# A block with Fourier mixing and a spatial gate on one core: chunks of the streamed operand made in pairs, operands moved to multiples of 512 bytes, element-wise work moved to VectorE

## The chip, the cores and the metric

One core of one Trainium2 chip runs the whole kernel. The metric is the device time of one launch in microseconds (us), median of several runs. TensorE does the matrix products, VectorE (DVE), ScalarE (ACT) and GpSimd (POOL) do element-wise work, SyncE (SP) issues most of the transfers. All data are fp32; matrix products run on fp32r operands.

## The reference

With x of 2048 x 512 (S x D), c of 512, and F/2 = 896 (FH):

```
mod = silu(c) @ w_mod, cut in six rows of 512: sa, ca, ga, sb, cb, gb
h = layernorm(x) * (1 + ca) + sa
x = x + ga * (Cr @ (h @ Hr^T) - Ci @ (h @ Hi^T))          # Cr, Ci 2048 x 2048; Hr, Hi 512 x 512
h = layernorm(x) * (1 + cb) + sb
z = gelu(h @ w_in)                                         # 2048 x 1792, halves z1, z2 of 896
g = w_sp @ layernorm(z2) + b_sp[:, None]                   # w_sp 2048 x 2048
out = x + gb * ((z1 * g) @ w_out)                          # w_out 896 x 512
```

## The kernel before

**Three matmuls for one.** Every operand is split in a high part rounded to fp32r and the rest (lo = value - high). `matmul3` (L93) issues three matmuls: high x high (L95), a second (L96) and a third (L97) with one low part each. The high part is made on ACT (L201 for the streamed operand), the low part by a DVE subtraction (L210).

**Chunks.** All streamed matrices go through one pipeline of 272 chunks of 128 x 512. A block of four chunks is loaded by SP into a `stage` tile (two buffers, L159). `prep_hi` (L184) turns one chunk with a DVE transpose in 32 x 32 squares (L173, or L193 in the z2 stage) into a tile `t` (two buffers) and has ACT copy it to `ah` (four buffers); `prep_lo` (L206) subtracts on DVE into `al` (three buffers). The loop calls `prep(n)` (L177) ahead of the matmuls of chunk n: it makes t and ah of chunk n + 3 and al of chunk n + 2. When a block's fourth chunk has been turned, its buffer is given to block b + 2.

**Stages**, in order of n, 16 to 128 chunks each:
- `mm_a` (L376), chunks 0 to 127: gp = h^T @ Cr^T (or Ci^T), 12 matmuls for one chunk; h is stationary, the chunk moves. The first four chunks (L387) run all high parts first. After each of the eight sums the result is split into `gh`, `gl` (pool `gtpool`).
- `mm_y` (L464), among them: y = g @ H, `gh` and `gl` stationary (128 columns of a 512-wide tile at a time), `hth`/`htl` moving: 384 matmuls. The rows mod 1 and 0 are folded into H through three small column tiles `col0..2` of 4 floats, which lie in pool `htpool` (L265 to L286).
- `mm_z1` (L522), 16 chunks of 21 matmuls: w_in's first half stationary.
- `mm_z2` (L538), 16 chunks of 24 matmuls of 448 columns: the chunk is stationary, w_in's second half moves, in two halves of 448 columns that lie behind one another in tiles of 896.
- `mm_w` (L618), 112 chunks: w_sp @ z2 in seven block products (Strassen's scheme), in the order 1, 6, 7, 4, 5, 3, 2, 16 chunks (eight k by two r) each. Products 1, 6, 4 and 2 take 12 matmuls for one chunk, 7, 5 and 3 take 9. They add up in PSUM banks `4 r + f`; 1, 5 and 2 start anew ("fresh"). After the last k of 1, 6, 7 and 4, `keep_w` (L633) copies banks to SBUF on ACT; after 5, 3 and 2, `add_w` (L642) adds them to such a copy on DVE. Product 4 needs `sum_t14` (L600) on DVE.
- `mm_o` (L709), the tail: 16 tiles of 21 matmuls, u = z1 * g split (L686, L692) as moving or stationary parts, then `add_o` (L704) adds x and stores.

**What sets the order.** The program is emitted by hand; each engine runs its own instructions in that order. `at(n, f, ...)` (L123) hangs a function on step n, and `run(n)` (L126) emits it behind the matmuls of that step (in the z stages ahead of them). On POOL run `add_bs` (L654, adds b_sp to g), `scale_wo` (L671, w_out times gb), a few others and the stores of intermediate results. `load_wo` (L667) has two buffers, and comes in products 3 and 2; `load_z1` (L658) brings z1 back, `make_u` (L663) multiplies on DVE.

**Where tiles lie.** Pools are stacked from both ends of SBUF. On the right come `edge` (which ends at a multiple of 512 bytes), `htpool`, `rows`, `gtpool`. A tile of 4 floats takes 32 bytes, so the three columns put 96 bytes into `htpool`: in the built program `gh0_0_0` starts at byte 142240 = 277 x 512 + 416, `ones_r` at 189344 = 369 x 512 + 416, while `hth0_1` (189952 = 371 x 512), `ah`, `hh`, `wih` and `uh` start at multiples of 512. `lines` (L72) is a tile that only takes room.

Of the kernel before, what the change touches and what calls it, by code (L numbers as in the profile page):

```python
# [13 lines left out]
P = 128  # L14
EPS = 1e-5
LINES = 160
# [3 lines left out]
def fnet_gmlp_kernel(  # L20
# [125 lines left out]
    stage, T, AH, AL = {}, {}, {}, {}  # L146
# [28 lines left out]
    prepared = set()  # L175

    def prep(n):  # L177

        if n not in prepared:
            prepared.add(n)  # L180
            prep_hi(n + 3)
            prep_lo(n + 2)

    def prep_hi(n, eng=None):  # L184
        if n >= NE:
            return
        b, k = divmod(n, 4)
        T[n] = blocks.tile([P, Q], F32, tag="t", bufs=2, name=f"t{n}")
        if n >= N4:
            squares(T[n], stage[b][:, k % 2], k // 2)  # L190
        elif N3 <= n < N4:

            nc.vector.transpose(T[n].rearrange("p (k a i) -> p a k i", k=4, i=32),  # L193
                                stage[b][:, :, 32 * k:32 * k + 32].rearrange("p (a k) i -> p a k i", k=4))
        else:
            squares(T[n], stage[b], k)
        AH[n] = blocks.tile([P, Q], F32R, tag="ah", bufs=4, name=f"ah{n}")
        if eng:
            eng.tensor_scalar(AH[n], T[n], 1.0, None, op0=ALU.mult)
        else:  # L200
            nc.scalar.activation(AH[n], T[n], AF.Copy)  # L201
        if k == 3:
            stage.pop(b)
            load(b + 2)

    def prep_lo(n):  # L206
        if n >= NE:
            return
        AL[n] = blocks.tile([P, Q], F32R, tag="al", bufs=3, name=f"al{n}")
        nc.vector.tensor_tensor(AL[n], T.pop(n), AH[n].bitcast(F32), op=ALU.subtract)  # L210
# [42 lines left out]
    WB, WT, COL = {}, {}, {}  # L253
# [11 lines left out]
    def load_columns(j):  # L265
        pl, tag = (hpre, "hraw") if j else (spool, "wb")
        WB[j] = pl.tile([P, 16, P], F32, tag=tag, bufs=1, name=f"wb{j}")
        load_block(WB[j], quad(w_mod, 0, j))
        COL[j] = htpool.tile([P, ND], F32, name=f"col{j}")

    def weigh_column(j, k):
        pl, tag = (spool, "wt") if k % 2 else (rows, "y")
        WT[j, k] = pl.tile([P, D], F32, tag=tag, bufs=1, name=f"wt{j}_{k}")
# [8 lines left out]
    def scale_columns():  # L282
        col = COL[1]
        nc.vector.tensor_scalar(col, col, 1.0, None, op0=ALU.add)
        COL[2] = htpool.tile([P, ND], F32, name="col2")
# [228 lines left out]
    def make_wi(e, k):  # L514
        wi_hi[e, k] = wpool[1 - e].tile([P, FH], F32R, name=f"wih{e}_{k}")
        wi_lo[e, k] = wpool[1 - e].tile([P, FH], F32R, name=f"wil{e}_{k}")
# [21 lines left out]
    def mm_z2(ns):  # L538
# [6 lines left out]
        for q in range(8):  # L545
            r, e = divmod(q, 2)
            ts, cols = slice(r * P, (r + 1) * P), slice(e * ZP, (e + 1) * ZP)
            for k, th, tl in a:
                matmul3(ZT[q][:, :ZP], th[:, ts], tl[:, ts], wi_hi[1, k][:, cols], wi_lo[1, k][:, cols],
# [68 lines left out]
    def mm_w(n):  # L618
# [11 lines left out]
        if k == 7:  # L630
            {1: keep_w, 6: keep_w, 7: keep_w, 4: keep_w}.get(p, add_w)(p, r)

    def keep_w(p, r):  # L633
# [5 lines left out]
        for f in range(G[p, r].shape[1]):  # L639
            nc.scalar.activation(G[p, r][:, f, :], GW[r, f], AF.Copy)  # L640

    def add_w(p, r):  # L642

        g = G[{5: 7, 3: 6, 2: 1}[p], r]
        for f in range(g.shape[1]):
# [8 lines left out]
    def add_bs(p, r, f):  # L654
        g = G[p, r][:, f, :]
        nc.gpsimd.tensor_tensor(g, g, wor["bs", r if p in (1, 6) else 2 + r], op=ALU.add)  # L656

    def load_z1(p, r):  # L658
        f0, f1 = (0, 4) if p in (1, 4) else (4, NF)
        Z1T[p, r] = gpool[0].tile([P, 4, Q], F32, tag="z1t", bufs=2, name=f"z1t{p}_{r}")[:, :f1 - f0]  # L660
# [6 lines left out]
    def load_wo(f):  # L667
        wor[f] = opool[0].tile([P, D], F32, tag="wor", bufs=2, name=f"wor{f}")
        nc.sync.dma_start(wor[f], w_out[f * P:(f + 1) * P, :])

    def scale_wo(f):  # L671
        nc.gpsimd.tensor_tensor(wor[f], wor[f], mods[5], op=ALU.mult)

    def make_wo(f):
        wo_hi[f] = opool[0].tile([P, D], F32R, name=f"woh{f}")
        wo_lo[f] = opool[0].tile([P, D], F32R, name=f"wol{f}")
# [63 lines left out]
    hi_h(0)  # L740
    prep_hi(0, nc.vector)
    prep_lo(0)
    lo_h(0)
    norm_x(1)
    hi_h(1)
    prep_hi(1)
    stats_first(2)
    prep_lo(1)
    lo_h(1)
    norm_x(2)  # L750
    prep_hi(2)
    hi_h(2)
    stats_first(3)
    norm_x(3)
    at(0, lo_h, 2)
# [59 lines left out]
    for t in range(NQ):  # L815
        n = 8 * NQ * (t + 1)
        for i in range(4):
# [37 lines left out]
    def change_s():  # L855
        p2.close()
        spre.append(ctx.enter_context(pool("spre", "right")))
        bpool.append(ctx.enter_context(pool("bpool", "right")))

# [5 lines left out]
    at(N2 + 5, change_s)  # L865
# [22 lines left out]
    zpool.append(ctx.enter_context(pool("zpool1", "right")))  # L888
# [23 lines left out]
    opool = []  # L912

    def change_g():
        wstack.close()
        gpool.append(ctx.enter_context(pool("gpool")))
        load_bs()
# [6 lines left out]
    for r in range(2):  # L924
        for f in range(4):
            at(NB[6] + 2 + 4 * r + f, add_bs, 1, r, f)
            at(NB[5] + 2 + 8 * r + 2 * f, add_bs, 4, r, f)
            if f < 3:
                at(NB[7] + 2 + 3 * r + f, add_bs, 6, r, f)
                at(NB[4] + 2 + 3 * r + f, add_bs, 7, r, f)  # L930
    at(NB[3] + 1, change_o)
    at(NB[2] - 10, load_z1, 4, 0)
    at(NB[2] - 9, load_z1, 7, 0)
    for f in range(4):
        at(NB[2] - 2 + f, make_u, 4, 0, f)
        at(NB[2] + 6 + f, make_u, 4, 1, f)
        if f < 3:
            at(NB[2] + 3 + f, make_u, 7, 0, f)
            at(NB[2] + 11 + f, make_u, 7, 1, f)
    at(NB[2] + 3, load_z1, 4, 1)  # L940
    at(NB[2] + 7, load_z1, 7, 1)
    for f in range(NF):
        n = NB[3] + 2 + 2 * f
# [72 lines left out]
```

## Time and profile before

| what | before |
|---|---|
| time, median of 3 runs | 965.48 us (965.05 to 965.58) |
| span of the profiled execution | 963.8 us |
| PE busy | 953.3 us (4196 matmuls) |
| DVE busy | 691.8 us |
| ACT busy | 369.6 us |
| POOL busy | 219.0 us |
| bytes moved | 161.27 MB |

The span runs from the first to the last instruction of one profiled execution; the page gives no other time of it. The runs' median is 1.7 us longer than this span. Matmuls are pipelined: one is listed with some 0.39 us, but the next starts sooner, so that the distance between starts ("pitch" below) is what a matmul costs. In a timeline row, the bracket at the end is the idle time before the instruction and who ended it.

### The profile page before, as it was taken

The page shows a single profiled execution, that of the slowest core. Times are in us where ns is not written, and L with a number is a line of the kernel's source. Part 1 is how long each engine was busy: PE and PEld are TensorE (multiplying, and loading weights), DVE is VectorE, ACT ScalarE, POOL GpSimd, SP SyncE. Part 2 cuts the span into 40 slices and gives each one's busy share as a digit, 9 for nine tenths or more (in the row PEclk, how much of TensorE's full clock was granted, in tenths as well). Part 3 has the DMA queues.
Part 4 walks back from the last instruction along what each step waited for, and adds up shares of the span by engine and source line. Part 5 has one row for each costly group of instructions (what it writes and reads, how often), then busy time and mean ns, then how long its engine had stood idle before and what let it go on. Part 6 is the DMA issues. An engine that isn't in the chain of part 4 may idle for free.

```text
span 963.8 us, 12355 instructions
## 1 busy us (share of the span) xinstructions
PE 953.3 (99%) x4196; PEld 788.8 (82%) x4196; DVE 691.8 (72%) x1085; ACT 369.6 (38%) x630; POOL 219.0 (23%) x363
## 2 busy tenths in 40 slices
PE   8999999999999999999999999999999999999998
PEld 5888888888888888888888999888888888778886
DVE  7789957785566767856555576888689698897642
ACT  4594424231232212322344356643444444342221
POOL 2330000111520345114323343213304230210000
PEclk9999999999999999999999999999999999999999
DMA  9996652666446787994678964545454456764441
GB/s 212 221 212 133 130 137 62 175 172 165 133 110 148 222 252 226 286 241 111 211 279 295 278 219 126 131 110 120 100 120 100 98 123 165 184 171 178 130 149 60
DMA packets 249535, 161.27 MB, mean 167 GB/s; under 512 B 130176, under 2 KB 218240, under 8 KB 249344
## 3 DMA queue, kind: packets, MB, share of 16 engines
q1 hardware_dynamic: 236800, 122.72, 53.1%
q0 software_dynamic: 11424, 37.24, 10.7%
q8 instruction: 33, 0.54, 0.2%
q10 hardware_dynamic: 1248, 0.52, 0.2%
q14 instruction: 30, 0.25, 0.1%
HBM read 123.73 MB, written 36.70 MB: 166 GB/s over the span
## 4 chain that ended last, share of the span: by engine, by line
PE 93%; DVE 3%; DMA 2%; issue 1%; SPq 1%; ACT 0%; POOL 0%; ACTq 0%; DVEq 0%
PE gp L95 12%; PE gp L96 12%; PE gp L97 12%; PE gw L97 8%; PE gw L96 8%; PE gw L95 8%; PE yp L96 3%; PE yp L95 3%; PE yp L97 3%; PE z2p L97 3%; PE z2p L96 3%; PE z2p L95 3%; PE z1p L96 3%; PE op L97 3%; PE z1p L97 3%; PE op L95 3%
## 5 line engine op out<-in xcount | busy, mean ns | idle before, releaser
L201 ACT ACTIVATE ah<-t 128x512 fp32r<-128x512 f32 x271 | 171.4, 632 | 452.9 <-DVE t L173 259.6
L210 DVE TENSOR_TENSOR al<-t,ah 128x512 fp32r<-128x512 f32 x272 | 192.9, 709 | 135.7 <-PE gp L96 50.4
L95 PE MATMUL gp<-ah,hh 128*128 128x512 f32 x496 | 193.3, 390 | 0.0
L96 PE MATMUL gp<-al,hh 128*128 128x512 f32 x496 | 193.3, 390 | 0.0
L97 PE MATMUL gp<-ah,hl 128*128 128x512 f32 x496 | 193.2, 389 | 0.0
L173 DVE STREAM_TRANSPOSE t<-stage 128x512 f32<-128x512 f32 x256 | 180.3, 704 | 11.3 <-DMA stage<-in_A_dft_seq_re_dram 5.0
L97 PE MATMUL gw<-ah,bl 128*128 128x512 f32 x400 | 156.6, 392 | 1.2 <-DVE bl L616 1.2
L95 PE MATMUL gw<-ah,bh 128*128 128x512 f32 x400 | 156.3, 391 | 1.0 <-DVE g L646 1.0
L96 PE MATMUL gw<-al,bh 128*128 128x512 f32 x400 | 156.4, 391 | 0.4 <-DVE al L210 0.4
L95 PEld LDWEIGHTS gp<-ah,hh 128*128 128x128 f32 x496 | 93.1, 188 | 19.9
L97 PEld LDWEIGHTS gp<-ah,hl 128*128 128x128 f32 x496 | 93.1, 188 | 19.7
L96 PEld LDWEIGHTS gp<-al,hh 128*128 128x128 f32 x496 | 93.1, 188 | 19.4
L97 PEld LDWEIGHTS gw<-ah,bl 128*128 128x128 f32 x400 | 75.4, 189 | 18.0 <-DVE bl L616 2.3
L95 PEld LDWEIGHTS gw<-ah,bh 128*128 128x128 f32 x400 | 75.5, 189 | 17.0 <-ACT woh L677 1.4
L96 PEld LDWEIGHTS gw<-al,bh 128*128 128x128 f32 x400 | 75.4, 189 | 16.7 <-DVE al L210 0.8
L656 POOL TENSOR_TENSOR g<-g,bs 128x512 f32<-128x512 f32 x28 | 44.4, 1619 | 118.0 <-ACT g L640 118.0
L588 POOL DMA_DIRECT2D s_d<-sj x64 | 35.3, 551 | 125.1 <-DVE sj L580 92.4
L96 PE MATMUL yp<-htl,gh 128*128 128x512 f32 x128 | 51.1, 399 | 0.0
L95 PE MATMUL yp<-hth,gh 128*128 128x512 f32 x128 | 50.4, 394 | 0.0
L97 PE MATMUL yp<-hth,gl 128*128 128x512 f32 x128 | 50.1, 392 | 0.0
L96 PE MATMUL z2p<-wil,ah 128*128 128x448 f32 x128 | 46.7, 365 | 0.0
L95 PE MATMUL z2p<-wih,ah 128*128 128x448 f32 x128 | 46.7, 365 | 0.0
(148 smaller groups left out, 1341.4 us busy)
## 6 DMA issues: line engine op xcount, KB each, us to landing
stage<-in_A_dft_seq_im_dram SPq DMA_DIRECT2D x64, 256.0 KB, 5.3
sj<-in_B_w_sp_dram SPq DMA_DIRECT2D x32, 512.0 KB, 7.5
s_d<-sj POOLq DMA_DIRECT2D x64, 256.0 KB, 3.9
stage<-s_d SPq DMA_DIRECT2D x128, 128.0 KB, 2.8
stage<-in_A_dft_seq_re_dram SPq DMA_DIRECT2D x60, 256.0 KB, 4.8
stage<-in_B_w_sp_dram SPq DMA_DIRECT2D x96, 128.0 KB, 3.3
stage<-h_d SPq DMA_DIRECT2D x32, 256.0 KB, 5.6
z_d<-z POOLq DMA_DIRECT2D x28, 256.0 KB, 8.0
```

The costliest lines, as they stand in the source:

```text
L95: nc.tensor.matmul(acc, ah, bh, start=first, stop=False, skip_group_check=go_on)
L96: nc.tensor.matmul(acc, ah, bl, start=False, stop=False, skip_group_check=go_on)
L97: nc.tensor.matmul(acc, al, bh, start=False, stop=last, skip_group_check=go_on)
L173: nc.vector.transpose(dst.rearrange("p (b i) -> p b i", i=32), block[:, :, 32 * k:32 * k + 32])
L201: nc.scalar.activation(AH[n], T[n], AF.Copy)
L210: nc.vector.tensor_tensor(AL[n], T.pop(n), AH[n].bitcast(F32), op=ALU.subtract)
L588: nc.gpsimd.dma_start(s_d[m, r, g][b * P:(b + 1) * P, :], a)
L656: nc.gpsimd.tensor_tensor(g, g, wor["bs", r if p in (1, 6) else 2 + r], op=ALU.add)
```

## The change

- **Pairs.** `t`, `ah` and `al` become three fixed tiles `ts` (2 slots), `ahs` and `als` (4 slots each). At odd n, `turn_two` turns chunks n + 3 and n + 4 with one DVE transpose (two in the z2 stage); at every n ACT makes ah of n + 3; at even n one DVE subtraction of 128 x 1024 makes al of n + 2 and n + 3. A block's buffer is handed on one step earlier. The first four chunks are turned one by one ahead of the loop, chunk 3 among them, so that the first pair's subtraction (chunks 2 and 3) is emitted at n = 0.
- **Places.** The columns move from `htpool` to `cpool`, and `lines` shrinks from 160 to 64 bytes, which keeps what follows in `cpool`'s stack at its place. w_in's second half is laid out as two halves in slots of 512 floats. `z1rows` moves to the right stack, `wt` to the ring of `rows`, `z1t` to `opool`, and w_out's tiles to a pool `wopool` of their own.
- **Engines.** b_sp: for products 7 and 4, `keep_w` becomes a DVE addition of the PSUM bank and b_sp (14 instructions) instead of an ACT copy with a POOL addition; for 1 and 6 the addition (14) runs on DVE in the tail. `scale_wo` (7) runs on DVE.
- **Times.** w_out is loaded, scaled and split during product 6. `make_u` of 4 and 7: the half r = 0 late in product 2, the half r = 1 in the first steps of the tail; the last `add_w` of product 2 also moves into the tail.
- **Banks.** Product 5 uses banks 3 r + f, product 2 uses 6, 7, 0, 1 for r = 0 and 2 to 5 for r = 1, the tail 6 and 7.

```diff
-LINES = 160
+LINES = 64
...
     def prep(n):
         if n not in prepared:
             prepared.add(n)
+            if n % 2:
+                turn_two(n + 3)
             prep_hi(n + 3)
-            prep_lo(n + 2)
+            if n % 2 == 0:
+                prep_lo(n + 2)
+
+    def slot(n, m=1):
+        return ts[:, n % 2:n % 2 + m, :]
...
+    def turn_two(n):
+        if n >= NE:
+            return
+        b, k = divmod(n, 4)
+        st = stage[b]
+        if n >= N4:
+            nc.vector.transpose(slot(n, 2).rearrange("p r (b i) -> p r b i", i=32),
+                                st[:, :, :, 16 * k:16 * k + 32])
+        elif n >= N3:
+            for m in range(k, k + 2):
+                nc.vector.transpose(slot(n + m - k)[:, 0].rearrange("p (k a i) -> p a k i", k=4, i=32),
+                                    st[:, :, 32 * m:32 * m + 32].rearrange("p (a k) i -> p a k i", k=4))
+        else:
+            nc.vector.transpose(slot(n, 2).rearrange("p k (b i) -> p k b i", i=32),
+                                st[:, :, 32 * k:32 * k + 64].rearrange("p b (k i) -> p k b i", k=2))
+        if k == 2:
+            stage.pop(b)
+            load(b + 2)
...
+        AH[n] = ahs[:, n % 4, :]
...
-    def prep_lo(n):
+    def prep_lo(n, m=2):
         if n >= NE:
             return
-        AL[n] = blocks.tile([P, Q], F32R, tag="al", bufs=3, name=f"al{n}")
-        nc.vector.tensor_tensor(AL[n], T.pop(n), AH[n].bitcast(F32), op=ALU.subtract)
+        lo = als[:, n % 4:n % 4 + m, :]
+        nc.vector.tensor_tensor(lo, slot(n, m), ahs[:, n % 4:n % 4 + m, :].bitcast(F32), op=ALU.subtract)
...
-    WB, WT, COL = {}, {}, {}
+    WB, WT = {}, {}
+    COL = {j: cpool.tile([P, ND], F32, name=f"col{j}") for j in range(3)}
...
+        if e:
+            wi_hi[e, k], wi_lo[e, k] = [wpool[0].tile([P, 2, 512], F32R, name=f"wi{m}{e}_{k}")[:, :, :ZP] for m in "hl"]
...
-                GW[r, f] = bank(4 * r + f, f"gw{p}_{r}_{f}")
+                k_ = 4 * r + f if p == 1 else 3 * r + f if p == 5 else (6, 7, 0, 1, 2, 3, 4, 5)[4 * r + f]
+                GW[r, f] = bank(k_, f"gw{p}_{r}_{f}")
...
-            nc.scalar.activation(G[p, r][:, f, :], GW[r, f], AF.Copy)
+            if p in (1, 6):
+                nc.scalar.activation(G[p, r][:, f, :], GW[r, f], AF.Copy)
+            else:
+                nc.vector.tensor_tensor(G[p, r][:, f, :], GW[r, f], wor["bs", 2 + r], op=ALU.add)
...
-        nc.gpsimd.tensor_tensor(wor[f], wor[f], mods[5], op=ALU.mult)
+        nc.vector.tensor_tensor(wor[f], wor[f], mods[5], op=ALU.mult)
...
     norm_x(3)
+    turn_one(3)
+    stage.pop(0)
+    load(2)
     at(0, lo_h, 2)
...
-    at(NB[2] - 10, load_z1, 4, 0)
-    at(NB[2] - 9, load_z1, 7, 0)
+    at(NB[3] + 3, load_z1, 4, 0)
+    at(NB[3] + 4, load_z1, 7, 0)
...
-        n = NB[3] + 2 + 2 * f
-        at(n, load_wo, f)
-        at(n + 4, scale_wo, f)
-        at(n + 6, make_wo, f)
-        at(n + 7, make_wo_lo, f)
+        n = NB[6] + 2 * f
+        at(n - 4, load_wo, f)
+        at(n + 1, scale_wo, f)
+        at(n + 1, make_wo, f)
+        at(n + 2, make_wo_lo, f)
     order = [(t, i) for t in (2, 3, 0, 1) for i in range(4)]
+    later = {0: [(make_u, 4, 1, 0), (make_u, 4, 1, 1), (add_w, 2, 0, [2])],
+             1: [(make_u, 4, 1, 2), (make_u, 4, 1, 3), (add_w, 2, 0, [3]), (load_z1, 1, 0)],
+             2: [(make_u, 7, 1, 0), (make_u, 7, 1, 1), (make_u, 7, 1, 2), (load_z1, 6, 0)],
+             3: [(add_w, 2, 1, [0, 1])], 4: [(add_w, 2, 1, [2, 3])]}
+    for n, p, r in ((3, 1, 0), (5, 6, 0), (7, 1, 1), (9, 6, 1)):
+        for f in range(4 if p == 1 else 3):
+            later.setdefault(n + f // 2, []).extend([(add_bs, p, r, f), (make_u, p, r, f)])
...
-        mm_o(*order[o], o % 2)
+        mm_o(*order[o], 6 + o % 2)
```

More of the change, by code (lines that the diff above doesn't have):

```diff
@@ L175, in fnet_gmlp_kernel @@
     prepared = set()
+    ts = blocks.tile([P, 2, Q], F32, name="ts")
+    ahs = blocks.tile([P, 4, Q], F32R, name="ahs")
+    als = blocks.tile([P, 4, Q], F32R, name="als")
     def prep(n):
@@ L514, in make_wi @@
     def make_wi(e, k):
-        wi_hi[e, k] = wpool[1 - e].tile([P, FH], F32R, name=f"wih{e}_{k}")
-        wi_lo[e, k] = wpool[1 - e].tile([P, FH], F32R, name=f"wil{e}_{k}")
+        if e:
+            wi_hi[e, k], wi_lo[e, k] = [wpool[0].tile([P, 2, 512], F32R, name=f"wi{m}{e}_{k}")[:, :, :ZP] for m in "hl"]
+            wraw[e, k] = wraw[e, k].rearrange("p (h f) -> p h f", h=2)
+        else:
+            wi_hi[e, k], wi_lo[e, k] = [wpool[1].tile([P, FH], F32R, name=f"wi{m}{e}_{k}") for m in "hl"]
         nc.scalar.activation(wi_hi[e, k], wraw[e, k], AF.Copy)
@@ L858, in change_s @@
         bpool.append(ctx.enter_context(pool("bpool", "right")))
+        zpool.append(ctx.enter_context(pool("zpool1", "right")))
+        zrow.append(w0.enter_context(pool("z1rows", "right")))
     def change_q():
```

114 lines of the change are left out of this document (44 added, 70 removed).

## The prediction

> **What bounds the kernel now.** I read the head of the page, then its chain, then TensorE's waits, then its timeline.
>
> ```profile
> span 963.8 us, 12355 instructions
> PE 953.3 (99%) x4196; PEld 788.8 (82%) x4196; DVE 691.8 (72%) x1085; ACT 369.6 (38%) x630; POOL 219.0 (23%) x363
> ```
>
> ```profile
> PE 93%; DVE 3%; DMA 2%; issue 1%; SPq 1%; ACT 0%; POOL 0%; ACTq 0%; DVEq 0%
> ```
>
> TensorE is busy 99% of the span and is 93% of the chain. So only two things shorten this kernel: a smaller distance between the starts of matmuls (the pitch), or fewer holes. DVE work that is merely saved is worth nothing unless a hole ends on it.
>
> ```profile
> PE gw L97 <- DVE bl L616: 1.2, 2, 1.0
> PE gw L95 <- DVE g L646: 1.0, 1, 1.0
> ```
>
> ```profile
> 606.17 0.39 PE L95 MATMUL gw<-ah,bh 128*128 128x512 f32 x1
> 700.09 0.39 PE L95 MATMUL gw<-ah,bh 128*128 128x512 f32 x1
> 703.49 0.39 PE L95 MATMUL gw<-ah,bh 128*128 128x512 f32 x1
> 839.53 0.63 PE L95 MATMUL gw<-ah,bh 128*128 128x512 f32 x1
> 841.66 0.63 PE L97 MATMUL gw<-ah,bl 128*128 128x512 f32 x1
> 883.75 0.39 PE L95 MATMUL op<-woh,uh 128*128 128x512 f32 x1
> ```
>
> The rows 700.09 and 703.49 are 15 matmuls apart: pitch 226.7 ns. The 1200 matmuls of the products would take 272.0 us at that pitch. They take 883.75 - 606.17 = 277.6 us, so 5.5 us are lost there. The waits give only 2.6 us of it; the rest is after-effect: behind the hole at product 2's start the pitch is 426 ns (839.53 to 841.66, five matmuls), nearly double, for about 3 us.
>
> Why is DVE late there? From the timelines of SP, DVE and POOL:
>
> ```profile
> 829.78 3.16 SPq L669 DMA_DIRECT2D wor<-in_B_w_out_dram  x2
> 832.99 4.84 SPq L157 DMA_DIRECT2D stage<-in_B_w_sp_dram  x8
> 833.50 0.71 DVE L173 STREAM_TRANSPOSE t<-stage 128x512 f32<-128x512 f32 x1 [0.94 <-DMA stage<-in_B_w_sp_dram]
> 833.87 1.30 POOL L672 TENSOR_TENSOR wor<-wor,mod 128x512 f32<-128x512 f32 x1 [6.21 <-DMA wor<-in_B_w_out_dram]
> 834.14 1.58 DVE L210 TENSOR_TENSOR al<-t,ah 128x512 fp32r<-128x512 f32 x1
> ```
>
> SP stands in front of `load_wo`, whose two buffers are still in use, and the stage loads queue behind it: a transpose waits for data. Then a subtraction runs beside POOL's `scale_wo` and takes 1.58 us. Alone it takes 0.6:
>
> ```profile
> 858.26 0.68 DVE L680 TENSOR_TENSOR wol<-wor,woh 128x512 fp32r<-128x512 f32 x1
> 858.86 0.70 DVE L173 STREAM_TRANSPOSE t<-stage 128x512 f32<-128x512 f32 x1
> 859.49 0.65 DVE L210 TENSOR_TENSOR al<-t,ah 128x512 fp32r<-128x512 f32 x1
> ```
>
> (DVE pitches 0.60 and 0.63 us.) Last, product 2 starts in the very banks that product 3's additions must first empty (the wait on L646 above).
>
> **Part 1, places of operands.** The pitch of other matmuls:
>
> ```profile
> 430.14 0.24 PE yp L96
> 432.94 0.24 PE yp L96
> ```
>
> The first two are pieces of the chain in order of time; the next two are groups of instructions:
>
> ```profile
> L95 PE MATMUL gp<-ah,hh 128*128 128x512 f32 x496 | 193.3, 390 | 0.0
> L303 PE MATMUL modp<-ws,ones_r 128*128 128x512 f32 x4 | 1.6, 394 | 0.0
> ```
>
> yp: 2.80 us for 12 matmuls, 233.3 ns, so 6.6 more than 226.7. Its moving `hth` starts at a multiple of 512 bytes; its stationary `gh` starts 416 behind one, because of the columns. modp, moving aligned and stationary `ones_r` off by 416, is long too (394 against 390). gp, gw and op, with both aligned, are not. So I blame the stationary operand's place. With the columns gone `gh` lies at a multiple of 512: 384 x 6.6 ns = **-2.5 us** (bounds 0 and -2.5).
>
> ```profile
> 344.97 0.40 PE L95 MATMUL gp<-ah,hh 128*128 128x512 f32 x1
> 347.73 0.39 PE L95 MATMUL gp<-ah,hh 128*128 128x512 f32 x1
> ```
>
> The 12 gp matmuls right behind a yp group take 2.76 us instead of 2.72. If that is yp's echo, some 16 such places give **-0.6 us** (bounds 0 and -1).
>
> ```profile
> 528.35 0.36 PE L95 MATMUL z2p<-wih,ah 128*128 128x448 f32 x1
> ```
>
> z2p: from here to 606.17 (above) there are 384 matmuls, 202.7 ns each. 448/512 of 226.7 would be 198.4. Half of them move columns that start 1792 = 3 x 512 + 256 bytes in. No row shows aligned 448 columns; bounds 0 and 384 x 4.3 ns = -1.6 us. If the half that is off costs the 6.6 ns of yp, it is 192 x 6.6 = **-1.2 us**; I take that.
>
> **Part 2, pairs.** The wide subtraction is nearly shown by one of 896 columns (its line: min/median/max in ns):
>
> ```profile
> L520 DVE TENSOR_TENSOR wil<-wraw,wih x8: 1079/1093/2182, 440.9 to 511.5; 128x896 fp32r<-128x896 f32 x8
> ```
>
> Adding 128 columns at the slope between 512 (0.69) and 896 (1.09): 1.23 us, pitch about 1.13, against 2 x 0.60. The wide transpose no row shows; between 1.13 and two single ones, 1.26; I take 1.16. So a pair saves some 0.17 us of DVE, 22 us over 128 pairs, all of it beside a busy TensorE: **0**. What matters is when the pair is ready. Two chunks later is the deadline, but the odd chunk's ah must now exist first:
>
> ```profile
> 703.73 0.63 ACT L201 ACTIVATE ah<-t 128x512 fp32r<-128x512 f32 x1 [0.93 <-PE gw L97]
> ```
>
> ACT starts 0.24 us after step n begins (703.49), since ah's slot is that of chunk n - 1. Then 0.63 + 0.05, then DVE 1.13: the pair is done 2.05 us after step n begins. Chunk n + 2 needs it two steps after that: 4.08 us in nine-matmul steps, 5.44 in twelve. Slack 2.2 and 3.6 us (the first start of al itself comes one matmul later). Queued behind the waiting subtraction are `lo_b`, evacuations and the next transpose. In mm_a (twelve-matmul steps, DVE with less than before) this holds. **0**, except at the start.
>
> **The start.** Before:
>
> ```profile
> 15.63 1.11 POOL L331 TENSOR_SCALAR first<-first 128x1 f32<-128x1 f32 x1
> 16.45 1.09 PE L387 MATMUL gp<-al,hh 128*128 128x512 f32 x4
> 16.78 0.82 ACT L119 ACTIVATE xn<-x,first 128x511 f32<-128x511 f32 x1 [1.43 <-POOL first L331]
> 17.50 0.62 ACT L201 ACTIVATE ah<-t 128x512 fp32r<-128x512 f32 x1
> 18.69 1.20 PE L387 MATMUL gp<-ah,hh 128*128 128x512 f32 x4 [0.23 <-ACT hh L363]
> 21.54 0.39 PE L95 MATMUL gp<-ah,hh 128*128 128x512 f32 x1
> ```
>
> TensorE needs al of chunk 2 at 16.45. After, that subtraction is one with chunk 3's, whose ah ACT makes behind the normalisation of row tile 3 (16.78), which waits for POOL. With DVE idle by then I give POOL's L331 0.3 us instead of 1.11, so the normalisation starts at 15.95, ah of chunk 3 ends at 17.3, the pair at 18.6. TensorE waits 2.2 us; the old hole ahead of 18.69 closes (0.4). **+1.8 us** at 21.54. Bounds: 0.5 (if the early chunks run ahead) and 3.6 (if the pitch doubles for 3 us behind this hole, as it did at 839).
>
> **Part 3, the products.** When can an evacuation start?
>
> ```profile
> 798.59 0.69 DVE L210 TENSOR_TENSOR al<-t,ah 128x512 fp32r<-128x512 f32 x1 [0.60 <-PE gw L96]
> 799.49 2.05 DVE L646 TENSOR_TENSOR g<-gw,g 128x512 f32<-128x512 f32 x3 [0.21 <-PE gw L97]
> ```
>
> The step begins about 798.55; the first bank is ready 0.9 later, the others 0.68 apart. In each place I count from the start of the last product's step k = 7, r = 0.
> - 4 to 5 (four banks now on DVE): pair to 2.05, four additions to 4.45, `lo_b` 4.92 (needed 5.9), transpose 6.08, four additions to 8.48 (bank 5 free at 7.28, needed 8.8), next pair 9.61 (needed 9.75), `lo_b` 10.08 (needed 9.97): 0.15 late.
> - 7 to 4 (three banks on DVE, and `sum_t14`, two additions of 0.6, in between): the same count gives the pair at 9.73 against 9.75 and `lo_b` at 10.33 against 9.97: 0.4 late.
> - 5 to 3: 0.3 late. 3 to 2: with banks 6, 7, 0, 1 free in time, 0.
> - What is late next: `lo_b`, each time. Together 0.85, and 0.15 for slow matmuls behind the holes: 1.0 us left of 5.5. **-4.5 us** (bounds 0 and -5.5).
>
> This counts 14 + 7 instructions more on DVE in the products at 0.6 us, and none on POOL, so no subtraction of 1.6 us. `load_wo`, moved into product 6, still blocks SP, since its buffer comes free two steps later.
>
> ```profile
> stage<-s_d SPq DMA_DIRECT2D x128, 128.0 KB, 2.8
> ```
>
> A stage block is asked for six steps of 2.72 us ahead of its transpose, 16.3 us. SP is held for two of them (5.4), takes 4.8 for the eight issues (832.99 above), and 2.8 until the last has landed: 3.3 us to spare; without that cover DVE waits, then TensorE after its slack of 3.6. In the tail a tile takes TensorE 21 x 0.2267 = 4.76 us; its own split and addition take DVE 1.7, so 3.1 are left, five instructions of 0.6. Tiles 3 and 4 get six, tile 5 four, tile 6 two: 1.2 us behind at most; the next split is due about 1.9 us later. z1's last blocks (transfers by line):
>
> ```profile
> z1t<-z_d SPq DMA_DIRECT2D x4, 1024.0 KB, 7.9
> ```
>
> are asked for about 3.6 us into tile 1 and land, 0.4 + 7.9 later, 2.4 us into tile 3, where they are used 4.1 us in: hidden by 1.7 us, then by the 1.9. **0** (bound +2).
>
> **Sum.** -2.5 - 0.6 - 1.2 + 1.8 - 4.5 = **-7.0 us**: the span goes from 963.8 to 956.8. I carry the difference of 1.7 us between span and median over unchanged: **958.5 us**.
>
> **Rivals.**
> - *Alignment buys nothing* (the change doesn't do what it says). yp may be slow for its mixture with gp, and z2p for its length. For it: two rows of modp are a thin proof, and z2p's off half doesn't stand out. Against: op, equally mixed in length and aligned, keeps 226.7. It takes away 4.3 us: 962.8. The Trainium skill ("SBUF — State Buffer", Specifications) knows lines of 16 bytes, within which accesses run at full bandwidth; 416 and 256 are multiples of 16, so by that page the move is worth nothing. Its "TensorE: Matmul & The Clock Gate" (Wait — 56ns, not 53.3ns?) gives one warm pitch, columns over 2.4 GHz plus 2.5 ns, 215.7 ns for 512, whatever the place; this trace has 226.7 and 233.3 for the same 512 columns, so the measurement decides against that one already.
> - *The hole only moves.* DVE now empties banks at 7 to 4 and 4 to 5, where my counts have margins of 0.02 to 0.15 us. If each DVE step costs 10% more than I took, each of the four places is some 1 us late, and the pitch doubles behind one of them as at 839: the 4.5 us stay lost, 963.0.
> - *Slower: the shared tile.* Slots of ts, ahs and als are now parts of one tile. If waits are kept for the whole tile, chunk n at even n waits for the pair emitted just ahead of it, 2.05 us at each of 136 pairs: +279 us, about 1240. It decides from the first even step. Against: ACT and POOL already work on slices of one `g`:
>
> ```profile
> 723.01 1.67 ACT L640 ACTIVATE g<-gw 128x512 f32<-128x512 f32 x3
> 723.66 9.66 POOL L656 TENSOR_TENSOR g<-g,bs 128x512 f32<-128x512 f32 x6 [24.98 <-ACT g L640]
> ```
>
> POOL starts when the first of ACT's three slices is done, not the last.
>
> **How the numbers follow.** Forecast 62%; alignment nothing 13%; hole moves 13%; both of these 4% (967); shared tile 4%; the rest 4%, half of it slower. About 0.2%, 1.9 us, can be told from no change; faster means under 963.5. Forecast and alignment rival are faster (the latter in part), the moved hole faster or same: faster 0.83, same 0.08, slower 0.09. Range: below, all bounds good but one, 958.5 - 1.3 (start) - 1.0 (no hole) - 0.8 (echo, z2p) = 955.4; above, the two rivals at 963.2.
>
> **What would show it.** yp and modp at 390 ns instead of 394 and more; z2p's stretch 1.2 us shorter; product 2 starting without a hole and no doubled pitch there; the wide subtraction at 1.23 us and the wide transpose at 1.2; POOL without L656 and L672, and no al over 1.3 us in the products; al at the start ready at 18.6. Wrong, if TensorE waits for al in steady steps, if lo_b's delays at 7 to 4 exceed 1 us, or if the first chunks wait longer than 2.2 us.

## The result and the profile after

The changed kernel is **slower** by 1.5%: 980.29 us median of 4 runs (980.10 to 981.29) against 965.53 us (965.05 to 966.29) for the kernel before beside it, a ratio of 1.0153 with a 95% interval of 1.0139 to 1.0167. The prediction said 958.5 us, with a range of 955.4 to 963.2. The head of the page of after:

```profile
span 979.5 us, 11882 instructions
PE 956.3 (98%) x4196; PEld 786.5 (80%) x4196; DVE 663.8 (68%) x859; ACT 351.4 (36%) x616; POOL 164.3 (17%) x328
```

VectorE and GpSimd have less to do (691.8 to 663.8 us, 219.0 to 164.3), and yet the span is 15.7 us longer. TensorE's waits in after say on what (the first five rows):

```profile
PE gp L96 <- DVE als L229: 5.8, 5, 1.7
PE gw L97 <- DVE bl L639: 3.6, 3, 1.7
PE gp L97 <- DVE hl L388: 2.0, 1, 2.0
PE gp L407 <- DVE als L229: 2.0, 1, 2.0
PE z1p L95 <- ACT z L558: 0.9, 1, 0.9
```

Columns: who waits for whom, us in total, times, the longest. `als` (the subtractions of a pair) and `hl` in mm_a are new; before, mm_a had no wait behind its first chunks. VectorE's groups of instructions show the reason (last column: idle time ahead of them, and what ended it); first after's, then the same group of before:

```profile
L229 DVE TENSOR_TENSOR als<-ts,ahs 128x1024 fp32r<-128x1024 f32 (+1 forms) x137 | 167.2, 1221 | 210.5 <-ACT ahs L223 209.7
L210 DVE STREAM_TRANSPOSE ts<-stage 128x1024 f32<-128x1024 f32 x70 | 86.6, 1237 | 0.9
```

```profile
L210 DVE TENSOR_TENSOR al<-t,ah 128x512 fp32r<-128x512 f32 x272 | 192.9, 709 | 135.7 <-PE gp L96 50.4 <-PE gw L96 28.7 <-PE z1p L96 27.9
```

Before, VectorE's idle time ahead of a subtraction ends on TensorE: VectorE was ahead and waited for a free slot of al, which costs nothing. After, nearly all of it ends on ScalarE's rounded copy: 209.7 us over 137 pairs, 1.5 us each. VectorE is not short of time; it stands.

Where the 15.7 us arise is read by putting the two traces side by side, matmul by matmul (both hold 4196 records in the same order). This table gives the start of the 61st, 521st, 1946th, 2691st and 4191st matmul minus that of before, in us, for after and for the kernels of the next section. The places are 22 us (behind the first chunks), 127 (where yp begins), 453 (where z1 begins), 613 (early in product 1) and 958 us.

| kernel | 22 | 127 | 453 | 613 | 958 |
|---|---|---|---|---|---|
| after | 1.9 | 13.8 | 10.4 | 11.6 | 15.7 |
| e8_narrow_pair_order | 1.1 | 1.0 | -2.5 | -2.5 | -7.7 |
| e7_pairs_old_order | 0.4 | 1.3 | -2.2 | -1.3 | -4.9 |
| e10_wide_turn_narrow_sub | 1.8 | 6.0 | 2.5 | 3.4 | -1.9 |
| e9_narrow_turn_wide_sub | 3.2 | 6.8 | 3.3 | 3.5 | 1.0 |
| e11_odd_copy_on_DVE | 0.6 | 1.8 | -1.5 | -0.3 | -1.7 |
| e2_singles | -0.1 | -0.2 | -3.7 | -3.6 | -9.1 |
| e4_places | 0.3 | 0.2 | -3.3 | -3.1 | -4.1 |

After loses 1.9 at the start and 11.9 more in mm_a before yp begins, wins 3.4 in the stretch of yp, loses 1.2 at z1 and 4.1 in the products. In the stretch of yp, mm_a's chunks go on in pairs with yp's matmuls between them, and after wins there what the places alone win (e4 3.5). One of mm_a's holes, on VectorE, ScalarE and TensorE in after:

```profile
74.21 1.24 DVE L210 STREAM_TRANSPOSE ts<-stage 128x1024 f32<-128x1024 f32 x1
75.37 0.65 DVE L388 TENSOR_TENSOR hl<-xn,hh 128x512 fp32r<-128x512 f32 x1
79.18 1.23 DVE L229 TENSOR_TENSOR als<-ts,ahs 128x1024 fp32r<-128x1024 f32 x1 [3.16 <-ACT ahs L223]
80.32 0.68 DVE L388 TENSOR_TENSOR hl<-xn,hh 128x512 fp32r<-128x512 f32 x1
...
81.30 1.25 DVE L210 STREAM_TRANSPOSE ts<-stage 128x1024 f32<-128x1024 f32 x1
```

```profile
75.54 0.63 ACT L223 ACTIVATE ahs<-ts 128x512 fp32r<-128x512 f32 x1 [0.47 <-DVE ts L210]
76.08 0.62 ACT L383 ACTIVATE hh<-xn 128x512 fp32r<-128x512 f32 x1
76.60 0.71 ACT L363 ACTIVATE xn<-x,sums 128x512 f32<-128x512 f32 x1
...
77.31 0.62 ACT L358 ACTIVATE xn<-x 128x512 f32<-128x512 f32 x1
...
77.92 0.62 ACT L301 ACTIVATE wt<-wt 128x512 f32<-128x512 f32 x1
...
78.53 0.61 ACT L223 ACTIVATE ahs<-ts 128x512 fp32r<-128x512 f32 x1
...
82.63 0.63 ACT L223 ACTIVATE ahs<-ts 128x512 fp32r<-128x512 f32 x1 [2.08 <-DVE ts L210]
```

```profile
78.35 0.39 PE L95 MATMUL gp<-ahs,hh 128*128 128x512 f32 x1
80.46 0.50 PE L96 MATMUL gp<-als,hh 128*128 128x512 f32 x1 [1.72 <-DVE als L229]
```

This is a **ring**. The transpose of a pair (74.21) lets ScalarE round the even chunk (75.54). The odd chunk's copy comes only at 78.53, since the fills of a whole step (the work that `at` hangs on it) stand ahead of it on ScalarE's queue: four passes with the reads of their sums, 2.45 us. VectorE stands 3.16 us for it, makes the pair (79.18), and with it the *even* chunk's al, which TensorE is waiting for at 80.46. Behind it on VectorE stands the next pair's transpose (81.30), and for that ScalarE now waits 2.08 us. This round takes 7.09 us; TensorE's two steps take 24 x 0.2267 = 5.44. The rounds differ with their fills: between the places 22 and 127 of the table two steps take 6.1 us on average (104.4 + 11.9 us for 460 matmuls). Each engine waits for the other in turn, and neither can work ahead. (The Trainium skill, "PSUM — Partial Sum Buffer", section "Engine vs sequencer instructions", says that these engines' queues are strictly first in, first out. The trace agrees: the copy at 78.53 needs nothing that came after 75.45, and starts only when the last fill ahead of it is done.)

In a product with nine-matmul steps the ring is bare; VectorE, then ScalarE:

```profile
810.50 1.24 DVE L203 STREAM_TRANSPOSE ts<-stage 128x1024 f32<-128x1024 f32 x1
813.04 1.23 DVE L229 TENSOR_TENSOR als<-ts,ahs 128x1024 fp32r<-128x1024 f32 x1 [1.30 <-ACT ahs L223]
814.18 0.55 DVE L639 TENSOR_TENSOR bl<-z,bh 128x384 fp32r<-128x384 f32 x1
814.65 1.24 DVE L203 STREAM_TRANSPOSE ts<-stage 128x1024 f32<-128x1024 f32 x1
```

```profile
811.86 1.15 ACT L223 ACTIVATE ahs<-ts 128x512 fp32r<-128x512 f32 x2 [2.58 <-DVE ts L203]
```

Transpose, two copies, subtraction, `lo_b`: 814.65 - 810.50 = 4.15 us, against 18 x 0.2267 = 4.08 of TensorE. Late work is never made up for, and the additions out of PSUM at each change of product come on top. TensorE at the changes from product 7 to 4, from 5 to 3 and from 3 to 2 (its idle time in brackets):

```profile
739.82 0.47 PE L95 MATMUL gw<-ahs,bh 128*128 128x512 f32 x1 [0.47 <-DVE g L672]
741.53 0.50 PE L97 MATMUL gw<-ahs,bl 128*128 128x512 f32 x1 [1.00 <-DVE bl L639]
```

```profile
819.17 0.47 PE L95 MATMUL gw<-ahs,bh 128*128 128x512 f32 x1 [0.46 <-DVE g L678]
820.74 0.50 PE L97 MATMUL gw<-ahs,bl 128*128 128x512 f32 x1 [0.87 <-DVE bl L639]
```

```profile
856.24 0.50 PE L97 MATMUL gw<-ahs,bl 128*128 128x512 f32 x1 [1.71 <-DVE bl L639]
```

### The profile page after: what moved, and what is told of

The parts are those of the page before. It is cut to its first block, busy times and chain, and to the rows that moved or that the text cites. A ratio compares the mean times of both kernels' runs of the same rounds, so it can differ in the third digit from the quotient of the medians.

```text
span 979.5 us, 11882 instructions
## 1 busy us (share of the span) xinstructions
PE 956.3 (98%) x4196; PEld 786.5 (80%) x4196; DVE 663.8 (68%) x859; ACT 351.4 (36%) x616; POOL 164.3 (17%) x328
## 4 chain that ended last, share of the span: by engine, by line
PE 41%; issue 4%; POOL 3%; DVE 3%; ACT 1%; DMA 0%; POOLq 0%; DVEq 0%; ACTq 0%
PE gw L97 9%; PE gw L95 8%; PE gw L96 8%; PE op L97 3%; PE op L95 3%; PE op L96 3%; PE z1p L95 2%; PE z1p L96 2%; PE z1p L97 2%; POOL s_d L611 1%; POOL rsz L108 1%; DVE als L229 1%; PE z2p L96 1%; PE z2p L97 1%; PE z2p L95 1%
## 5 line engine op out<-in xcount | busy, mean ns | idle before, releaser
L223 ACT ACTIVATE ahs<-ts 128x512 fp32r<-128x512 f32 x271 | 166.3, 628 | 472.9 <-DVE ts L210 215.8
L229 DVE TENSOR_TENSOR als<-ts,ahs 128x1024 fp32r<-128x1024 f32 (+1 forms) x137 | 167.2, 1221 | 210.5 <-ACT ahs L223 209.7
L96 PE MATMUL gp<-als,hh 128*128 128x512 f32 x496 | 194.6, 392 | 5.9 <-DVE als L229 5.8
L97 PE MATMUL gp<-ahs,hl 128*128 128x512 f32 x496 | 193.8, 391 | 2.0 <-DVE hl L388 2.0
L95 PE MATMUL gp<-ahs,hh 128*128 128x512 f32 x496 | 193.6, 390 | 0.0
L97 PE MATMUL gw<-ahs,bl 128*128 128x512 f32 x400 | 157.5, 394 | 3.8 <-DVE bl L639 3.6
L95 PE MATMUL gw<-ahs,bh 128*128 128x512 f32 x400 | 156.0, 390 | 0.9 <-DVE g L672 0.5
L96 PE MATMUL gw<-als,bh 128*128 128x512 f32 x400 | 156.0, 390 | 0.6 <-DVE als L229 0.6
L97 PEld LDWEIGHTS gp<-ahs,hl 128*128 128x128 f32 x496 | 93.5, 189 | 21.7 <-DVE hl L388 2.4
L210 DVE STREAM_TRANSPOSE ts<-stage 128x1024 f32<-128x1024 f32 x70 | 86.6, 1237 | 0.9
L203 DVE STREAM_TRANSPOSE ts<-stage 128x1024 f32<-128x1024 f32 x56 | 69.4, 1238 | 0.2
```

The lines of the kernel that those rows point to most:

```text
L95: nc.tensor.matmul(acc, ah, bh, start=first, stop=False, skip_group_check=go_on)
L96: nc.tensor.matmul(acc, ah, bl, start=False, stop=False, skip_group_check=go_on)
L97: nc.tensor.matmul(acc, al, bh, start=False, stop=last, skip_group_check=go_on)
L203: nc.vector.transpose(slot(n, 2).rearrange("p r (b i) -> p r b i", i=32), st[:, :, :, 16 * k:16 * k + 32])
L210: nc.vector.transpose(slot(n, 2).rearrange("p k (b i) -> p k b i", i=32), st[:, :, 32 * k:32 * k + 64].rearrange("p b (k i) -> p k b i", k=2))
L223: nc.scalar.activation(AH[n], slot(n)[:, 0], AF.Copy)
```

## The experiments

**First batch.** My theory 1 after the result: the *order* does it, the pair's subtraction made in the step of its odd copy, where before a subtraction used a copy one step old. Rival 2: the *width* of the instructions. Rival 3: the transfers. Rival 4: in the products the moved work, not the pairs. The kernel before took 965.59 us beside these.

e7_pairs_old_order, wide transposes, but single subtractions in the old order:

```
             if n % 2:
+                prep_lo(n + 2, 1)
                 turn_two(n + 3)
             prep_hi(n + 3)
             if n % 2 == 0:
-                prep_lo(n + 2)
+                prep_lo(n + 2, 1)
```

> The kernel after, but every subtraction made singly, one step behind its rounded copy as before (al n+2 at step n needs ah n+2 of the step before); the transposes stay in pairs. Theory 1 (the pair subtraction at the even step waits for ScalarE's copy of the same step, which stands behind that step's fills, and the next double transpose queues behind it): the loss of some 13.8 us up to the end of mm_a falls below 2 us, the slow drift in the products goes, in all 960 to 967 us. Rival 2 (the wide instructions themselves hold VectorE's other work back in blocks of 1.24 us): the double transposes stay, so at least half of the loss stays, 972 to 980 us. Rival 3 (stage buffers given back at another time, the transfers): 978 to 981 us.

Measured 960.21 us (959.35 to 960.73), ratio 0.9937 (0.9921 to 0.9954). Theory 1 came out; rivals 2 and 3 did not.

e8_narrow_pair_order, the pair's order with each wide instruction cut in two:

```
-        if n >= N4:
-            nc.vector.transpose(slot(n, 2).rearrange("p r (b i) -> p r b i", i=32),
-                                st[:, :, :, 16 * k:16 * k + 32])
...
+        for m in range(2):
+            if n >= N4:
+                squares(slot(n + m)[:, 0], st[:, m], k // 2)
...
-        lo = als[:, n % 4:n % 4 + m, :]
-        nc.vector.tensor_tensor(lo, slot(n, m), ahs[:, n % 4:n % 4 + m, :].bitcast(F32), op=ALU.subtract)
         for i in range(m):
-            AL[n + i] = lo[:, i, :]
+            AL[n + i] = als[:, (n + i) % 4, :]
+            nc.vector.tensor_tensor(AL[n + i], slot(n + i)[:, 0], ahs[:, (n + i) % 4, :].bitcast(F32), op=ALU.subtract)
```

> The kernel after, but each double transpose and each double subtraction written as two single instructions in the same places, so the order of the pairs without a wide instruction. Theory 1 (order and wait): 976 to 985 us, the loss of mm_a at least 8 us. Rival 2 (width): within 3 us of a kernel without the loss, 961 to 966 us.

Measured 957.86 us (957.78 to 957.92), ratio 0.9914 (0.9898 to 0.9929). Theory 1 as I had put it **fell**: the order alone costs 1.4 us against the single chunks (e2, below), 1.2 of them at the start. VectorE waits for ScalarE here too, 167.2 us in all for after's 209.7, without harm:

```profile
L228 DVE TENSOR_TENSOR als<-ts,ahs 128x512 fp32r<-128x512 f32 x272 | 184.5, 691 | 167.9 <-ACT ahs L221 167.2
```

e2_singles, chunks made as in before, all else as in after:

```
-            if n % 2:
-                turn_two(n + 3)
             prep_hi(n + 3)
-            if n % 2 == 0:
-                prep_lo(n + 2)
+            prep_lo(n + 2)
...
+        T[n] = blocks.tile([P, Q], F32, tag="t", bufs=2, name=f"t{n}")
+        AH[n] = blocks.tile([P, Q], F32R, tag="ah", bufs=4, name=f"ah{n}")
+        AL[n] = blocks.tile([P, Q], F32R, tag="al", bufs=3, name=f"al{n}")
```

> The kernel after with the chunks made one by one exactly as before; places, banks, b_sp, w_out's scale, evacuations on VectorE and u stay as after. Theory 1: before's 965.5, less 3.35 for the aligned places, plus about 1.1 at z1, plus what the copies out of PSUM on VectorE cost at the changes of product (at most 4), less 2.3 at product 2: 959 to 965 us. Rival 4 (the losses in the products come from the moved work and not from the pairs): the 7 us there stay, 967 to 970 us.

Measured 956.42 us (956.18 to 957.09), ratio 0.9900 (0.9884 to 0.9916): faster than either kernel and than any expectation. So rival 4 is out: without the pairs the products win 5.5 us instead of losing 4.1, and the pairs cost 980.29 - 956.42 = 23.9 us. Of TensorE's waits these three groups are left, all in the first 20 us:

```profile
PE gp L386 <- DVE ah L199: 2.5, 1, 2.5
PE busyp L291 <- DVE busy L231: 1.5, 1, 1.5
PE gp L386 <- ACT hh L362: 0.6, 2, 0.4
```

e4_places, before with the columns moved and nothing else:

```
-LINES = 160
+LINES = 64
...
-    WB, WT, COL = {}, {}, {}
+    WB, WT = {}, {}
+    COL = {j: cpool.tile([P, ND], F32, name=f"col{j}") for j in range(3)}
...
-        COL[j] = htpool.tile([P, ND], F32, name=f"col{j}")
...
-        COL[2] = htpool.tile([P, ND], F32, name="col2")
```

> The kernel before with nothing changed but the places: mod's columns in the constants' pool and the constants' pool shorter, so that gh, gl and ones_r start at a multiple of 512 bytes. The same pitch as after, 226.7 ns for 233.3 on yp's matmuls: 384 x 6.6 = 2.5 us and the echo on the chunks of that stretch, in all 961.9 to 962.6 us. If the gain on the yp rows is given back by the chunks behind them: 965 us. z2p's rows stay at 365 ns.

Measured 961.70 us (961.54 to 963.17), ratio 0.9959 (0.9946 to 0.9972). The gain is the places' own: 3.5 us by 453 us, as expected, and 0.9 more at the product 2 hole. The three groups of yp in e4:

```profile
L95 PE MATMUL yp<-hth,gh 128*128 128x512 f32 x128 | 49.8, 389 | 0.0
L96 PE MATMUL yp<-htl,gh 128*128 128x512 f32 x128 | 49.8, 389 | 0.0
L97 PE MATMUL yp<-hth,gl 128*128 128x512 f32 x128 | 49.8, 389 | 0.0
```

**Second batch.** Neither order nor width alone: so what is it that both together do? (The kernel before took 965.37 us beside these.) The theory now was the wide subtraction, which ties the even chunk's al to the odd chunk's ah.

e9_narrow_turn_wide_sub has only the transposes of e8's edit:

```
-        if n >= N4:
-            nc.vector.transpose(slot(n, 2).rearrange("p r (b i) -> p r b i", i=32),
-                                st[:, :, :, 16 * k:16 * k + 32])
...
+        for m in range(2):
+            if n >= N4:
+                squares(slot(n + m)[:, 0], st[:, m], k // 2)
...
```

> The kernel after, with each double transpose written as two single ones; the subtraction of the pair stays one wide instruction. Theory now (the wide subtraction binds al of the even chunk to ah of the odd one, which ScalarE copies behind a whole step's fills; with two single subtractions al of the even chunk is free of it): most of the loss stays, since only 0.6 us of the loop goes with the narrow transpose: 966 to 977 us. Rival (the two wide instructions together are too much of a block for VectorE, either one alone is not): 957 to 962 us.

Measured 966.01 us (964.99 to 967.78), ratio 1.0003 (0.9992 to 1.0013): on the edge of the expected range.

e10_wide_turn_narrow_sub has only the subtractions of it:

```
-        lo = als[:, n % 4:n % 4 + m, :]
-        nc.vector.tensor_tensor(lo, slot(n, m), ahs[:, n % 4:n % 4 + m, :].bitcast(F32), op=ALU.subtract)
         for i in range(m):
-            AL[n + i] = lo[:, i, :]
+            AL[n + i] = als[:, (n + i) % 4, :]
+            nc.vector.tensor_tensor(AL[n + i], slot(n + i)[:, 0], ahs[:, (n + i) % 4, :].bitcast(F32), op=ALU.subtract)
```

> The kernel after, with each double subtraction written as two single ones in the same place and order; the double transposes stay. Theory now: the even chunk's al no longer waits for the odd chunk's ah, 956 to 961 us, and mm_a without waits on als but at the start. Rival (the order of the pairs and the double transpose make the loop): 970 to 980 us.

Measured 963.65 us (962.74 to 964.33), ratio 0.9981 (0.9972 to 0.9991). A miss for both: mm_a still loses 4.3 us behind the start. The tie of even to odd isn't the whole. The four kernels make a square: both narrow 957.9, wide transpose alone 963.7 (+5.8), wide subtraction alone 966.0 (+8.2), both 980.3 (+22.4, 8.5 more than the sum). That fits a ring: a shorter round counts only until it is shorter than TensorE's two steps. The two narrow transposes let the even copy start sooner; the two narrow subtractions let the first of them run beside the odd copy. The traces show the rounds. In product 3 after's take 4.15 us. With either width alone they take 3.7, under TensorE's 4.08 (e9 3.69, e10 3.70; e8, with neither, 3.17), while VectorE catches up behind a change of product, and 4.08 once it has. Two rounds' starts in e10:

```profile
810.01 1.24 DVE L203 STREAM_TRANSPOSE ts<-stage 128x1024 f32<-128x1024 f32 x1
...
813.71 1.24 DVE L203 STREAM_TRANSPOSE ts<-stage 128x1024 f32<-128x1024 f32 x1
```

In the products e10 indeed loses nothing (from 613 us on it wins 5.2, as e8 does). The kernel e9 wins 2.5 there; what it still loses is not explained by the round. In mm_a, with 7.09 against 5.44 in a step with many fills, half a microsecond is not enough, so either width alone still loses some 4 us there.

e11_odd_copy_on_DVE leaves both wide instructions and their order and takes ScalarE out of the ring's second half:

```
-            prep_hi(n + 3)
+            prep_hi(n + 3, None if n % 2 else nc.vector)
```

> The kernel after with both wide instructions and the pair's order, but the odd chunk's rounded copy made by VectorE right ahead of the pair's subtraction (one instruction more on VectorE per pair, one less on ScalarE). Theory now (what the wide subtraction waits for is ScalarE's queue of fills): the wait goes although VectorE has more to do, 957 to 967 us. Rival (width, VectorE's throughput in blocks): the same or worse than after, 978 us and up.

Measured 963.89 us (962.86 to 965.18), ratio 0.9988 (0.9978 to 0.9997). This is the run that shows the cause in mm_a: 57.5 us of work more on VectorE, and 11.9 us of loss there become 1.2. VectorE hardly stands ahead of the pair any more (15.8 us for 210.5); ahead of the new copy TensorE is again what it waits for:

```profile
L229 DVE TENSOR_TENSOR als<-ts,ahs 128x1024 fp32r<-128x1024 f32 (+1 forms) x137 | 168.0, 1226 | 15.8 <-ACT ahs L223 3.6 <-DVE ahs L221 0.5
L221 DVE TENSOR_SCALAR ahs<-ts 128x512 fp32r<-128x512 f32 x136 | 57.5, 423 | 119.9 <-PE gp L97 40.2 <-PE z1p L97 30.4 <-PE gw L97 25.4
```

In the products, where no fill stands between the two copies, it helps less: it wins 1.4 us there where e8 wins 5.2. What the rest is was not followed up; e10 keeps the wide transposes and loses nothing there, so these alone are not it.

e12_singles_pool_back asks what won in the products: e2_singles with the additions, the scale (one step earlier than in e2) and the copies out of PSUM on their old engines:

```
-                nc.vector.tensor_tensor(G[p, r][:, f, :], GW[r, f], wor["bs", 2 + r], op=ALU.add)
+            nc.scalar.activation(G[p, r][:, f, :], GW[r, f], AF.Copy)
...
-        nc.vector.tensor_tensor(g, g, wor["bs", r], op=ALU.add)
+        nc.gpsimd.tensor_tensor(g, g, wor["bs", r if p in (1, 6) else 2 + r], op=ALU.add)
...
-        nc.vector.tensor_tensor(wor[f], wor[f], mods[5], op=ALU.mult)
+        nc.gpsimd.tensor_tensor(wor[f], wor[f], mods[5], op=ALU.mult)
```

> The kernel with single chunks and all else of after (e2_singles, 956.4 us), but b_sp's additions and w_out's scale back on GpSimd and the copies out of PSUM of products 7 and 4 back on ScalarE, as before; the new banks, the early load of w_out and the new u stay. If the gain in the products (5.4 us from 606 us on) comes from GpSimd no longer working beside VectorE (subtractions of 1.58 us): 959 to 962 us. If it comes from the early load of w_out (SyncE no longer in front of the stage loads at product 2) and the banks: 956 to 957.5 us.

Measured 957.25 us (957.02 to 957.68), ratio 0.9918 (0.9903 to 0.9933): all three moves together are worth 0.8 us, although the subtractions beside GpSimd are stretched again (up to 1.59 us).

**Third batch** (before: 965.08 us). e14_late_w_out, on e2_singles:

```
-        n = NB[6] + 2 * f
-        at(n - 4, load_wo, f)
-        at(n + 1, scale_wo, f)
-        at(n + 1, make_wo, f)
-        at(n + 2, make_wo_lo, f)
+        n = NB[3] + 2 + 2 * f
+        at(n, load_wo, f)
+        at(n + 4, scale_wo, f)
+        at(n + 6, make_wo, f)
+        at(n + 7, make_wo_lo, f)
```

> The single-chunk kernel (e2_singles, 956.4 us) with w_out loaded, scaled and split at the steps of before (products 3 and 2) in place of product 6 on; all else as there, the scale on VectorE. If the hole at product 2's start came from SyncE standing in front of load_wo with the stage loads behind it: the hole and the doubled pitch at 836 to 842 us come back, 959 to 961 us. If it came from GpSimd's scale beside VectorE: 956 to 957.5 us.

Measured 965.71 us (964.89 to 966.60), ratio 1.0006 (0.9996 to 1.0015): 9.3 us more than e2, at least twice what I expected, and not by before's way. Now the scale itself stands on VectorE's queue and waits for w_out, with transposes and subtractions behind it:

```profile
817.36 7.81 SPq L680 DMA_DIRECT2D wor<-in_B_w_out_dram  x2
```

```profile
822.31 0.69 DVE L683 TENSOR_TENSOR wor<-wor,mod 128x512 f32<-128x512 f32 x1 [6.11 <-DMA wor<-in_B_w_out_dram]
```

So a scale on VectorE needs the early load. That the early load is what won in before's hole follows only by leaving out the others (GpSimd at most 0.8, banks 0 below); before with the early load alone was not run, as the places of the pools change with it.

e15_old_banks, on e2_singles:

```
-                k_ = 4 * r + f if p == 1 else 3 * r + f if p == 5 else (6, 7, 0, 1, 2, 3, 4, 5)[4 * r + f]
-                GW[r, f] = bank(k_, f"gw{p}_{r}_{f}")
+                GW[r, f] = bank(4 * r + f, f"gw{p}_{r}_{f}")
...
-        mm_o(*order[o], 6 + o % 2)
+        mm_o(*order[o], o % 2)
```

> The single-chunk kernel (e2_singles, 956.4 us) with the products' PSUM banks numbered as before (product 2 starts in the banks that product 3's additions must empty first). If the banks were worth what before's wait on that line shows: 957.0 to 958 us, a wait of 0.5 to 1 us at product 2's start; with a doubled pitch behind it 959 to 960 us. If VectorE empties them in time once no load is late: 956.2 to 956.8 us.

Measured 956.45 us (956.20 to 956.92), ratio 0.9910 (0.9895 to 0.9924): the same as e2. The banks are worth nothing once no load is late.

e16_offset_256 and e17_offset_448 ask which places are slow: e4_places with a tile of 256 or 64 bytes beside the columns' old place (and the weighted columns' buffer taken from `rows`, as in after, which makes the room):

```
         load_block(WB[j], quad(w_mod, 0, j))
+        if j == 1:
+            htpool.tile([P, 64], F32, name="pad")
```

In e17 the 64 is 16.

> The kernel before with the places of e4_places, but 256 bytes put beside the columns, so that gh, gl and ones_r start 256 bytes past a multiple of 512 (before: 416 past; e4: 0). If only multiples of 512 are fast: yp's pitch 233.3 ns, 965 us. If multiples of 64 do: 226.7 ns, 962 us.

> As e16_offset_256 with 64 bytes, so gh, gl and ones_r start 448 bytes past a multiple of 512. Only multiples of 512 fast: yp's pitch 233.3 ns, 965 us. Multiples of 64 fast (416 is none): 226.7 ns, 962 us. In between: the cost goes with how many bytes lie over the line, some other pitch.

Single runs: 961.74 and 962.62 us. At 256 yp's pitch is 226.7 ns; at 448 it is 228.9 (384 starts to the next start, 87.0 and 87.9 us in all). So "only multiples of 512" is wrong, and "multiples of 64" too. yp's groups in e17:

```profile
L96 PE MATMUL yp<-htl,gh 128*128 128x512 f32 x128 | 50.4, 394 | 0.0
L95 PE MATMUL yp<-hth,gh 128*128 128x512 f32 x128 | 50.2, 392 | 0.0
L97 PE MATMUL yp<-hth,gl 128*128 128x512 f32 x128 | 49.7, 388 | 0.0
```

## Why the prediction was wrong, by its own steps

- **Part 2, pairs: forecast 0 beside the start's 1.8, they cost 23.9 us with it. This step failed.** I worked out a deadline for one pair: ScalarE starts 0.24 us after step n begins, the pair is done at 2.05, TensorE needs it at 4.08 or 5.44, slack 2.2 and 3.6. Every duration in it was right (the subtraction 1.23 us forecast and found, pitch 1.14; the transpose's pitch 1.16). But it assumes, without a row for it, that the pair's transpose and even copy are long done and that ScalarE is free. The transpose stands behind the last pair's subtraction on VectorE, that one behind a copy on ScalarE, and that behind ScalarE's fills and the last transpose. I followed the chain one pair back and not round to itself; the round is 4.15 us for 4.08 in the products, and 6.1 on average (7.09 in the one shown) for 5.44 in mm_a before yp. e8, e9 and e10 show it by shortening the ring and e11 by taking ScalarE's queue out of it. Of the signs of being wrong that I had named, the first is what happened: TensorE waits for al in steady steps of mm_a (five times, 5.8 us).
- **mm_a, "twelve-matmul steps, DVE with less than before. This holds."** The weakest sentence: it looked at VectorE's load, where nothing was short, and not at ScalarE's queue in the same steps. Half of the 23.9 us arose there.
- **The start, +1.8:** right in mechanism and size. TensorE waited 2.0 us for the first pair, and was 1.9 behind before at 22 us; TensorE went on at 18.80, where I said 18.6.
- **Part 1, -2.5 and the echo of -0.6:** right. After wins 3.4 us in that stretch, e4 3.5; yp's and modp's rows are at 389 ns. The rival of alignment that buys nothing fell, and with it what I had drawn from the lines of 16 bytes in the Trainium skill ("SBUF — State Buffer", Specifications). 416 and 448 are multiples of 16, as 0 and 256 are, and yet slower (233.3 and 228.9 ns for 226.7).
- **z2p, -1.2: wrong,** it is 0. Its rows are 365 ns before and after. The moving operand starting 256 bytes past a multiple of 512 costs nothing, and 202.7 ns is what 448 columns take here at either place. I had charged 256 bytes with the price of 416; for the stationary operand too 256 is free (e16).
- **Part 3, -4.5 (bounds 0 and -5.5):** right without the pairs (e2 wins 5.5 from 613 us on), lost with them: after loses 4.1. I had counted it with the margins of the pair's deadline, so it is luck that the size comes out for single chunks. My reason was right in one half: SyncE in front of `load_wo` mattered (e14 for the new kernel, by elimination for before), GpSimd beside VectorE only 0.8 us, the banks nothing.
- **z1:** not forecast. After loses 1.2 us there, and the others with wide transposes too (e7 0.9, e10 0.8, e11 1.1); with single ones it is 0 to 0.2 (e8, e9, e2). ScalarE, held up by the wide transposes, comes late to empty the first bank.
- **The tail, 0:** right. From 870 us on no matmul moves against before.
- **The rival "the hole only moves"** had the right place (product changes, `lo_b` late), and gave its worst case as 963. It missed for the same reason: it took the ring's margin for a margin at each change.
- **The rival "the shared tile"** had the right sign, slower, and another cause. e8 keeps the shared tiles and takes 957.9 us.

The sum of the right terms, -2.5 - 0.6 - 4.5, would have been 957.9 us with single chunks; e2 measures 956.4.

## What to carry to other kernels

When two engines pass a chunk back and forth, add up the whole round (A's work, B's queue ahead of its part, B's work, A's again, and what else stands on A before the next round) and compare it with the time that the bottleneck takes for as many chunks; slack against one deadline says nothing if the round is longer. An instruction of double width saves a start, but its first half is ready only when its second half's inputs are, and everything behind it moves by that; here it paid nowhere. Idle time ahead of an engine's instructions is harmless as long as the bottleneck ends it. When another helper starts to end it, look for a ring and compare its round with the bottleneck's time: in e8 the helper ends it too, and nothing is lost. Wide instructions with room for two pairs in `ts` were not tried.

## What the runs showed of the hardware

- TensorE's pitch depends on where the *stationary* operand (a row of 512 bytes) starts. 0 and 256 bytes past a multiple of 512 give 226.7 ns per 512-column matmul, 448 gives 228.9, 416 gives 233.3. In these runs the moving operand stays at a multiple of 512, so whether the place counts by itself or against the moving one is open. A moving operand 256 bytes past costs nothing (z2p); at 416 or 448 none was tried. What rule lies behind these four values was not tried. (The places follow from the order of the pools and the sizes of the tiles; no trace lists them.)
- A hole in TensorE's work may be followed by some matmuls at nearly double pitch. In after this happened behind the hole of 2.00 us, from 38.30 to 41.29 at 0.43 us a piece, 1.4 us more lost, and not behind the 1.72 us at 80.46 or the 1.97 us at 18.80. The size of one hole doesn't decide alone: in before it followed two holes of 1.04 and 1.00 us, 1.7 us apart (836.47 and 838.17). What decides was not tried. After's rows:

```profile
36.96 0.50 PE L97 MATMUL gp<-ahs,hl 128*128 128x512 f32 x1 [2.00 <-DVE hl L388]
...
38.30 0.63 PE L96 MATMUL gp<-als,hh 128*128 128x512 f32 x1
38.73 0.63 PE L97 MATMUL gp<-ahs,hl 128*128 128x512 f32 x1
...
40.86 0.63 PE L96 MATMUL gp<-als,hh 128*128 128x512 f32 x1
41.29 0.51 PE L97 MATMUL gp<-ahs,hl 128*128 128x512 f32 x1
```
